# Sliding-window attention and a gated MLP in one kernel: batches 2 to 7 in two-block runs over all heads, q and k turned by DMA into rings

## The chip, the cores and the metric

The kernel runs on one core of a Trainium2 chip. The metric is the device time of one execution in microseconds; the median of the runs is compared. The engines are named as the profile names them: PE (TensorE, matmuls) with PEld (its weight loads), DVE (VectorE), ACT (ScalarE), POOL (GpSimd) and SP (SyncE, which here only issues DMAs). SP and POOL each issue DMAs in the order of the program, and the same 16 DMA engines move all of them.

## The reference

Eight batches, eight heads, 576 positions, 64 numbers a head. Each position attends to itself and the 63 before it; the result goes through two matrices with h * cos(h) between them.

```python
scores = scale * np.matmul(q, k.transpose(0, 1, 3, 2))      # scale = 1/8
mask = (rel >= 0) & (rel < 64)                              # rel = query position - key position
attn = softmax(np.where(mask, scores, -1e9))
x = np.matmul(attn, v)  # to rows of 512: all heads of a position beside each other, 4608 rows
h = x @ w_in            # 512 x 2048
out = (h * np.cos(h)) @ w_out                               # 2048 x 512
```

Inputs and output are float32; the matmuls run on bf16 copies.

## The kernel before

**Units and tiles.** The 4608 rows of x are worked through in nine tiles of 512 rows (`mt` 0 to 8). A sequence of 576 positions is nine blocks of 64 queries, so a tile is eight blocks and a batch nine. Heads go in pairs: pair p holds heads 2p and 2p + 1 on the lower and upper 64 partitions. A *unit* is (batch b, pair p, block j); its scores are 128 rows (64 queries of each head of the pair) by 128 columns (the block's keys and those of the block before). Up to four units that share a PSUM bank are a *group*.

**A unit's way.** `g_scores` makes the scores in PSUM. `g_max` (DVE) adds the mask, writes s and takes the maximum of each row. `g_exp` (ACT) takes one exponential per unit with the sum beside it. `g_inv` (DVE) takes the reciprocals of a group's sums, `g_norm` (POOL, some on DVE) multiplies and writes bf16 weights `w`. `g_trans` has SP issue a DMA transpose to `wT` (groups in `direct` use TensorE instead). `values` multiplies `wT` with v, 64 matmuls per tile, and `put_x` copies the result out of PSUM to `xT`, the input of the MLP.

**Scores of batches 2 to 7.** One 128x128 matmul for each unit: the weights are a block-diagonal copy of q (`qblocks`: head 0's 64 columns above, head 1's below, zeros elsewhere), so one matmul serves both heads. q therefore needs to be turned (features to partitions) and spread into `qblocks`: `tr_q` turns chunks of 96 rows on TensorE and `put_block` copies twice for each pair, or `turn_q` has SP transpose a chunk and `put_turned` spreads it. `TURNED` says how many of the six chunks of a batch go by DMA: two in batches 4 to 6, six in batch 7, none in 2 and 3. k's six chunks are all turned by SP (`turn_k`). The zeros are set once, by eight DVE memsets in the head. Batches 0 and 1 use pairs of 64x64 matmuls on the plain `qtiles`.

**v.** `load_v` brings 128 rows at a time. A block's values need its own 64 rows of v and the 64 before; the tiles that straddle two loads are made by `spread_v`, two POOL copies per batch (DMAs or DVE in the first batches).

**A tile of the MLP.** First 16 steps of four matmuls (512 columns) make h's sixteen blocks in five PSUM banks in turn; after each, ACT takes `sin` of h + pi/2 and DVE multiplies (`gT`). Then 16 steps of four matmuls make the output, 4 x 128 rows, each accumulated over 16 blocks; the copies of the results (DVE, ACT, DVE, ACT) go to `out_sb`, and SP stores 256 rows (512 KB) at a time. The first three blocks of h are interleaved over the four pairs (`skewed`), so that h can begin when pair 0 of xT is there.

**What sets the order.** A tile has T = 32 plan units, one for each step of four matmuls; the first half makes h, the second the output. `at(time, step)` puts a step on the plan, and `pump(time)` emits everything due so far between two steps of matmuls. Each engine then runs its instructions in the order of emission and waits by semaphores. Tile 0 and the loads before it are written out by hand in `FIRST`.

**Where attention stood.** Tile t (1 to 6) does all 36 units of batch t + 1, from plan unit 14.6 on, `PACE` 0.36 units apart per unit of work; `LAGS` gives the due times of the later steps. Within a batch the blocks needed first come first (`CUTS`). The values of tile mt are due 1.01 units before its beginning, those of the last tile 8 units before. q and k for the next batch are loaded in twelve chunks between units 5.6 and 15 of the tile before; k's turns are due from 5.5 units before the tile on, v's loads at 0.5 to 4.5.

**Tables.** Sine and exponential use different ACT tables. `exp_table` loads that of the exponential after the last sine of tiles 1 to 6, the sine's comes with the next sine.

Of the kernel before, what the change touches and what calls it, by code (L numbers as in the profile page):

```python
# [10 lines left out]
def _safe_warn(msg, *a, **kw):  # L11
# [3 lines left out]
F32 = mybir.dt.float32  # L15
# [8 lines left out]
NU = 9  # L24
NC, NP = 6, 96
GF = 4
LAST = 384
PACE = 0.36
CUTS = (
# [6 lines left out]
)  # L36
# [4 lines left out]
LAGS = (0.2, 1, 3, 3.2, 3.8)  # L41
# [5 lines left out]
TURNED = {4: 2, 5: 2, 6: 2, 7: 6}  # L47
# [29 lines left out]
def kernel(  # L77
# [80 lines left out]

    def rows_tile(name):
        return ld.tile([128, NC * H * D], BF16, tag=name, name=name)  # L160

    def load_heads(name, b, p0=0, n=PAIRS):
        if (name, b) not in st:
            st[name, b] = rows_tile(name)[:, 0:PAIRS * RC * D].rearrange("p (a x) -> p a x", a=PAIRS)
# [494 lines left out]
```

## Time and profile before

| | us |
|---|---|
| median of three runs | 309.15 (308.91 to 309.35) |
| span of the profiled execution, first to last instruction | 308.3 |
| PE busy | 298.4 |
| ACT busy | 234.4 |
| DVE busy | 229.3 |
| POOL busy | 192.6 |

The profile is one execution. Its span leaves out what lies before the first and after the last instruction. "Busy" counts the time in which an engine's instructions run; a matmul's end is modelled, so where TensorE's time matters, the chain of work that ended last is used: it goes back from the last instruction, at each step to what released it or to the instruction ahead on its engine, and gives the place in time and the length of each piece. The view by windows gives every engine's busy time in a stretch. In the DMA rows, "to landing" is the time from SP's issue to the last byte's arrival. L numbers are lines of the kernel: L304 is the score matmul of batches 2 to 7, L310 that of batches 0 and 1, L220 the transposes of q on TensorE, L385 the values, L454 the matmuls of h, L619 those of the output, L337 the exponentials, L354 the product with the reciprocals, L368 the DMA transpose of w, L261 and L245 those of k and q, L183 and L189 the loads of q, k and v, L474 the stores. L138 is the line of a helper that makes every copy.

### The profile page before, as it was taken

What the parts mean: (1) busy time and instruction counts of PE and PEld (TensorE: products, weight loads), DVE (VectorE), ACT (ScalarE), POOL (GpSimd) and SP (SyncE); (2) the same over time, 40 slices, a digit from 0 to 9 for tenths busy, and PEclk for the clock granted to TensorE, in tenths of its full rate; (3) what the DMA queues carried; (4) which work ended last, traced back from release to release, by engine and by line L of the source; (5) the groups of instructions that cost most, each with busy time, mean ns of one, the idle gap of its engine ahead of it and who ended that gap; (6) DMA issues with size and microseconds to landing.
All of it is one profiled execution on the core that took longest, in us unless ns stands there. A gap on an engine that the chain in (4) does not pass through costs nothing.

```text
span 308.3 us, 7917 instructions
## 1 busy us (share of the span) xinstructions
PE 298.4 (97%) x2622; PEld 159.0 (52%) x2622; DVE 229.3 (74%) x909; ACT 234.4 (76%) x785; POOL 192.6 (62%) x228
## 2 busy tenths in 40 slices
PE   6978999999999999999999999999999999999996
PEld 3767854544555455445554545455545554454443
DVE  6897988689787976798579866987698768335701
ACT  5897699686997699769976998699869986116600
POOL 7898568996559758967998699949902940000000
PEclk9799999999999999999999999999999999999999
DMA  7999999999999994999999998999794634011011
GB/s 147 180 210 176 198 184 124 117 149 169 233 126 114 153 235 83 100 130 228 153 119 136 215 160 100 156 180 191 90 141 106 162 70 153 2 68 71 0 64 72
DMA packets 159945, 42.14 MB, mean 137 GB/s; under 512 B 148256, under 2 KB 155168, under 8 KB 159904
## 3 DMA queue, kind: packets, MB, share of 16 engines
q0 software_dynamic: 100192, 18.06, 81.9%
q1 hardware_dynamic: 59424, 23.09, 39.8%
q8 instruction: 20, 0.33, 0.5%
q10 hardware_dynamic: 288, 0.49, 0.4%
q14 instruction: 21, 0.17, 0.2%
HBM read 36.70 MB, written 9.44 MB: 150 GB/s over the span
## 4 chain that ended last, share of the span: by engine, by line
PE 88%; POOL 3%; DMA 3%; DVE 2%; ACT 2%; issue 1%; POOLq 0%; DVEq 0%; ACTq 0%
PE h_ps L454 35%; PE out_ps L619 35%; PE s_ps L304 4%; PE h_ps L418 4%; PE out_ps L437 4%; PE o_ps L385 3%; DMA k<-in_k_dram 3%; PE tq_ps L220 1%; PE out_ps L466 1%; ACT e L337 1%; POOL w L354 1%; POOL q L166 1%; DVE v L138 1%; PE s_ps L310 1%; PE tw_ps L365 1%
## 5 line engine op out<-in xcount | busy, mean ns | idle before, releaser
L619 PE MATMUL out_ps<-w_out,gT 128*128 128x512 bf16 x496 | 117.3, 379 | 0.0
L454 PE MATMUL h_ps<-xT,w_in 128*128 128x512 bf16 x512 | 115.3, 379 | 0.2
L605 ACT ACTIVATE sin<-h_ps 128x512 f32<-128x512 f32 x128 | 73.7, 598 | 32.7 <-PE h_ps L454 31.9
L608 DVE TENSOR_TENSOR gT<-h_ps,sin 128x512 bf16<-128x512 f32 x128 | 82.1, 685 | 21.9 <-ACT sin L605 21.2
L337 ACT ACTIVATE e<-s,negm 128x128 f32<-128x128 f32 (+1 forms) x256 | 97.1, 382 | 0.6 <-DVE negm L325 0.6
L354 POOL TENSOR_TENSOR w<-e,rden 128x512 bf16<-128x512 f32 (+1 forms) x74 | 70.2, 963 | 36.7 <-DVE rden L347 30.6
L454 PEld LDWEIGHTS <-w_in 128*128 128x128 bf16 x512 | 48.8, 98 | 54.8 <-issue 0.4
L619 PEld LDWEIGHTS <-gT 128*128 128x128 bf16 x496 | 45.9, 98 | 44.3
L325 DVE CUSTOM_DVE_ANT_0 s<-s_ps,mask 128x128 f32<-128x128 f32 (+1 forms) x256 | 56.4, 278 | 1.8 <-PE s_ps L310 0.9
L337 ACT ACTIVATION_READ_ACCUMULATOR e<-s,negm 128x1 f32 x256 | 48.1, 188 | 0.0
L189 POOL DMA_DIRECT2D v<-in_v_dram x40 | 34.4, 879 | 0.2 <-issue 0.2
L183 POOL DMA_DIRECT2D q<-in_q_dram x36 | 28.3, 785 | 8.9 <-DMA v<-in_v_dram 3.2
L183 POOL DMA_DIRECT2D k<-in_k_dram x36 | 28.0, 779 | 6.2 <-DMA k<-in_k_dram 3.0
L138 ACT COPY out_sb<-out_ps 128x512 f32<-128x512 f32 (+1 forms) x18 | 10.2, 565 | 24.5 <-PE out_ps L619 18.4
L347 DVE RECIPROCAL rden<-den 128x4 f32<-128x4 f32 (+1 forms) x79 | 13.1, 166 | 18.8 <-ACT e L337 18.5
L304 PEld LDWEIGHTS <-qB 128*128 128x128 bf16 x216 | 16.4, 98 | 14.2
L138 DVE CAST xT<-o_ps 128x512 bf16<-128x512 f32 x24 | 15.5, 677 | 10.2 <-PE o_ps L385 10.2
L138 DVE COPY out_sb<-out_ps 128x512 f32<-128x512 f32 x18 | 12.4, 690 | 13.2 <-PE out_ps L619 12.5
L304 PE MATMUL s_ps<-kT,qB 128*128 128x128 bf16 (+1 forms) x216 | 21.3, 217 | 0.0
L325 DVE DVE_READ_ACCUMULATOR2_ANT negm<- 128x1 f32 x256 | 21.3, 83 | 0.0
L138 POOL COPY v<-v 64x1536 bf16<-64x1536 bf16 (+3 forms) x12 | 18.8, 1570 | 0.3
L138 DVE COPY qB<-tq_ps 64x384 bf16<-64x384 bf16 (+1 forms) x40 | 15.5, 388 | 0.4
(73 smaller groups left out, 260.2 us busy)
## 6 DMA issues: line engine op xcount, KB each, us to landing
out_dram<-out_sb SPq DMA_DIRECT2D x16, 512.0 KB, 7.5
v<-in_v_dram POOLq DMA_DIRECT2D x32, 128.0 KB, 6.1
q<-in_q_dram POOLq DMA_DIRECT2D x36, 96.0 KB, 8.7
k<-in_k_dram POOLq DMA_DIRECT2D x36, 96.0 KB, 8.7
w_in<-in_moe_w_in_dram POOLq DMA_DIRECT2D x4, 512.0 KB, 9.1
w_out<-in_moe_w_out_dram POOLq DMA_DIRECT2D x4, 512.0 KB, 10.7
wT<-w SPq DMA_TRANSPOSE x68, 4.2
q<-in_q_dram POOLq DMA_DIRECT2D x7, 144.0 KB, 6.1
```

The costliest lines, as they stand in the source:

```text
L138: {"a": nc.scalar.copy, "p": nc.gpsimd.tensor_copy}.get(engine, nc.vector.tensor_copy)(out, in_)
L183: nc.gpsimd.dma_start(out=st[name, b][:, c].rearrange("p (h d) -> p h d", h=H), in_=src.rearrange("h p d -> p h d"))
L189: nc.gpsimd.dma_start(out=vt.rearrange("p (h d) -> p h d", h=H), in_=v[b, :, c * 128:c * 128 + n, :].rearrange("h p d -> p h d"))
L304: nc.tensor.matmul(out=s_ps[:, u, 0:64 * chunks].rearrange("p (a t) -> p a t", a=chunks), lhsT=qblocks[(b % 2) * PAIRS + p][:, j].rearrang ...
L325: nc.vector.tensor_tensor_reduce(out=s[:, u, c], in0=s_ps[:, u, c], in1=mask[:, 2 - j % 2 if j else 0, c], scale=-scale if b else -1.0, sc ...
L337: nc.scalar.activation(e[:, u, c], s[:, u, c], AF.Exp, bias=negm[:, u:u + 1], scale=1.0 if n < n_first else -1.0, accum_out=den[:, u:u + 1])
L347: nc.vector.reciprocal(out=rden[:, 0:len(groups[n])], in_=den[:, 0:len(groups[n])])
L354: (nc.gpsimd if engine == "p" else nc.vector).tensor_tensor(out=w[:, 0:u], in0=e[:, 0:u], op=ALU.mult, in1=rden[:, 0:u].unsqueeze(2).to_br ...
L454: nc.tensor.matmul(out=st["h", ff], lhsT=w_in_sb[:, ks, ff * 128:ff * 128 + 128], rhs=st["xT", mt][:, ks], start=start, stop=stop)
L605: nc.scalar.activation(sin, h_ps, AF.Sin, bias=math.pi / 2.0)
L608: nc.vector.tensor_tensor(out=gt[:, e], in0=h_ps, in1=sin, op=ALU.mult)
L619: nc.tensor.matmul(out=o_ps[e], lhsT=gT[ff // 2][:, ff % 2, ms * 128:ms * 128 + 128], rhs=w_out_sb[:, ff], start=ff == 0, stop=ff == n_ff - 1)
```

## The change

From batch 2 on the work is counted in *runs*: run r is the two blocks 2r and 2r + 1, counted through all batches, for all four pairs, so eight units. Tile t (1 to 7) does four runs, 32 units, from run 9 + 4(t - 1) on; tile 7 does the last three. The three first of a tile's runs are the last ones that the next tile's values need.

- q and k come in loads of 128 rows (`load_run`, two of 64 rows where a run crosses into the next batch), the next tile's eight in every tile, in six buffers each. SP turns each of them by DMA (`turn_run`) into `qring` and `kring`, which hold nine runs and are written over in turn. No q of these batches is turned on TensorE, and there is no block-diagonal copy any more: `qblocks`, its memsets, `put_block` and `put_turned` are gone.
- The scores of a run are two groups: pairs 0 and 2, pairs 1 and 3. `g_quads` makes both at once: for each of four units, four matmuls with 64x64 weights, one on each quarter of the array: head 0 and head 1 of the one pair to the lower and upper rows of the first bank, head 1 and head 0 of the other pair to the lower and upper rows of the second bank. So pairs 1 and 3 have their heads swapped, and `values` takes them swapped. The two banks come from the three-buffer pool `ps_t`, not from the h banks.
- v also has a ring, in 128-row loads, and a second one (`vW`) for the windows that straddle two loads, filled by two POOL copies per tile.
- The values of pairs 0 and 2 are due 2.05 units before the end of a tile, those of 1 and 3 1.05 units before; h takes the pairs in the order 0, 2, 1, 3. This also holds for the last tile.
- The sine's table is loaded ahead of h's matmuls by a step of its own, the exponential's after tile 7's sines too.
- In `FIRST` the memsets are gone, and the loads for batch 2 are runs 9 to 12.

```diff
+RING = 2 * NU
+RUN0, RUNS = 9, 4
+PAIR_ORDER = (0, 2, 1, 3)
+VALUES = (2.05, 1.05)
+SCORES = (11, 16.4, 19.4, 22.4)
+EXPS = tuple(15.6 + 1.6 * k for k in range(8))
+LAGS = (0.5, 1.9, 2, 3.4)
...
+    qring = const.tile([128, PAIRS, RING * 64], BF16, name="qT")
+    kring = const.tile([128, PAIRS, RING * 64], BF16, name="kT")
+    vD = const.tile([128, RING // 2, d_model], BF16, name="v")
+    vW = const.tile([128, RING // 2 - 1, d_model], BF16, name="vW")
...
+    def load_run(name, r):
+        st["run", name, r] = rows = ld.tile([128, H * D], BF16, tag="r" + name, name="r" + name, bufs=6)
+        load_rows({"q": q, "k": k}[name], rows, r)
+
+    def turn_run(name, r):
+        at_ = 128 * (r % NU)
+        nc.sync.dma_start(out={"q": qring, "k": kring}[name][:, :, at_:at_ + 128], in_=st.pop(("run", name, r)), transpose=True)
...
+    for r in range(RUN0, n_mt * TU // 2):
+        groups += [[(*divmod(g, NU)[:1], p, g % NU) for p in ps_ for g in (2 * r, 2 * r + 1)] for ps_ in ((0, 2), (1, 3))]
...
+    def g_quads(n):
+        banks = [ps_t.tile([128, GF, 128], F32, tag="t", name="s_ps") for _ in range(2)]
+        for u in range(GF):
+            for i, h, to in ((0, 0, 0), (0, 1, 1), (1, 1, 0), (1, 0, 1)):
+                b, p, j = groups[n + i][u]
+                d, e = slice(64 * h, 64 * h + 64), slice(64 * to, 64 * to + 64)
+                nc.tensor.matmul(out=s_of(banks[i][e, u], b, j), lhsT=q_of(b, p, j)[d], rhs=k_of(b, p, j)[d],
+                                 start=True, stop=True, skip_group_check=True)
+        st["s", n], st["s", n + 1] = banks
...
-            if b > 1:
-                nc.tensor.matmul(out=s_ps[:, u, 0:64 * chunks].rearrange("p (a t) -> p a t", a=chunks),
-                                 lhsT=qblocks[(b % 2) * PAIRS + p][:, j].rearrange("d h t -> d (h t)"), rhs=rhs,
-                                 start=True, stop=True, skip_group_check=True)
...
+                of = 1 - h if b >= 2 and p % 2 else h
                 nc.tensor.matmul(out=o_ps[64 * h:64 * h + 64, 64 * i:64 * i + 64],
+                                 lhsT=window(b, j)[:, 128 * p + 64 * h:128 * p + 64 * h + 64],
+                                 rhs=wT[:, 64 * of:64 * of + 64], start=True, stop=True, skip_group_check=True)
...
+    for t in range(1, B):
+        t0 = T * t
+        runs = [RUN0 + RUNS * (t - 1) + i for i in range(RUNS) if RUN0 + RUNS * (t - 1) + i < n_mt * TU // 2]
+        for i, r in enumerate(runs):
+            at(t0 + 0.5 + 2.5 * i, turn_run, "k", r)
+            at(t0 + 0.5 + 2.5 * i + 1.2, turn_run, "q", r)
+            at(t0 + 0.5 + i, load_v, r)
+            at(t0 + SCORES[i], g_quads, n)
+            for e in range(2):
+                k_ = 2 * i + e
+                at(t0 + SCORES[i] + LAGS[0] + 0.5 * e, g_max, n)
+                at(t0 + EXPS[k_], g_exp, n)
+                for lag, fn in zip(LAGS[1:], (g_inv, g_norm, g_trans)):
+                    at(t0 + EXPS[k_] + lag, fn, n)
+                n += 1
         for half_ in range(2):
+            at(t0 + 12.5 + 0.1 * half_, spread_v, half_, runs[0], runs[-1] + 1)
+        for i, r in enumerate(r + RUNS for r in runs):
+            if r < n_mt * TU // 2:
+                for e, name in enumerate("kq"):
+                    at(t0 + 4.5 + 1.8 * i + 0.9 * e, load_run, name, r)
     for mt in range(2, n_mt):
+        for i, p in enumerate(PAIR_ORDER):
+            time = T * mt - VALUES[i // 2] + 0.01 * i
+            at(time, values, mt, p)
+            at(time + 0.2, put_x, mt, p, "a" if i == 2 else None)
...
     for mt in range(1, n_mt):
...
+        pump(base - 0.5)
+        if mt > 1:
+            sine_table()
+        for n, ks in enumerate(PAIR_ORDER):
+            skewed(mt, ks, n)
...
-            if ff == n_ff - 1 and mt < B - 1:
+            if ff == n_ff - 1 and mt < B:
                 exp_table()
```

More of the change, by code (lines that the diff above doesn't have):

```diff
@@ L186, in load_v, with load_rows @@
[L186 to L202 removed]
+    def load_rows(of, to, r):
+        blocks = [divmod(g, NU) for g in (2 * r, 2 * r + 1)]
+        if blocks[0][0] == blocks[1][0]:
+            b, j = blocks[0]
+            parts = ((0, 128, b, 64 * j),)
+        else:
+            parts = tuple((64 * i, 64, b, 64 * j) for i, (b, j) in enumerate(blocks))
+        for at_, n, b, s0 in parts:
+            nc.gpsimd.dma_start(out=to[at_:at_ + n].rearrange("p (h d) -> p h d", h=H),
+                                in_=of[b, :, s0:s0 + n, :].rearrange("h p d -> p h d"))
@@ new lines, in load_v, with spread_v @@
+    def load_v(r):
+        load_rows(v, vD[:, r % NU], r)
+    def load_run(name, r):
[4 more added lines that the diff above has]
+        nc.sync.dma_start(out={"q": qring, "k": kring}[name][:, :, at_:at_ + 128], in_=st.pop(("run", name, r)), transpose=True)
+    def spread_v(half, lo, hi, engine="p"):
+        d = slice(64 * half, 64 * half + 64)
+        rs = [r for r in range(lo, hi) if r % NU]
+        while rs:
+            n = 1
+            while n < len(rs) and rs[n] % NU == rs[0] % NU + n:
+                n += 1
+            at_ = rs[0] % NU
+            rs = rs[n:]
+            to, of = vW[d, at_ - 1:at_ - 1 + n], vD[d, at_ - half:at_ - half + n]
+            if engine == "s":
+                nc.sync.dma_start(out=to, in_=of)
+            else:
+                copy(engine, to, of)
@@ L334, in g_exp @@
         den = att.tile([128, GF], F32, tag="den", name="den", bufs=8)
-        for u, (_, _, j) in enumerate(groups[n]):
-            c = slice(0, 128 if j or n < n_first else 64)
+        for u, (b, _, j) in enumerate(groups[n]):
+            c = slice(0, 128) if j or n < n_first else own(b, j)
             nc.scalar.activation(e[:, u, c], s[:, u, c], AF.Exp, bias=negm[:, u:u + 1], scale=1.0 if n < n_first else -1.0,
@@ L342, in g_inv @@
         e, den = st["e", n]
-        for u, (_, _, j) in enumerate(groups[n]):
+        for u, (b, _, j) in enumerate(groups[n]):
             if j == 0 and n >= n_first:
-                nc.vector.memset(e[:, u, 64:128], 0.0)
+                nc.vector.memset(e[:, u, own(b, j + 1)], 0.0)
         rden = att.tile([128, GF], F32, tag="rden", name="rden", bufs=8)
@@ L591 @@
         gT = []
-        for ks in range(PAIRS):
-            pump(max([base - 1] + [time for time, _, fn, args in plan if fn is put_x and args[:2] == (mt, ks)]))
-            skewed(mt, ks, ks)
+        pump(base - 0.5)
[3 more added lines that the diff above has]
+            skewed(mt, ks, n)
         for ff in range(n_ff):
-            for ks in range(PAIRS):
+            for n, ks in enumerate(PAIR_ORDER):
                 if ff >= SKEW:
-                    first(mt, ff, ks, ks == 0, ks == PAIRS - 1)
+                    first(mt, ff, ks, n == 0, n == PAIRS - 1)
             h_ps = st.pop(("h", ff))
```

199 lines of the change are left out of this document (42 added, 157 removed), and 45 rows, old and new, of tables (CUTS, FIRST).

## The prediction

> **What bounds the kernel now.** I read the page first: the busy shares, then the chain of work that ended last.
>
> ```profile
> span 308.3 us, 7917 instructions
> PE 298.4 (97%) x2622; PEld 159.0 (52%) x2622; DVE 229.3 (74%) x909; ACT 234.4 (76%) x785; POOL 192.6 (62%) x228
> ...
> PE 88%; POOL 3%; DMA 3%; DVE 2%; ACT 2%; issue 1%; POOLq 0%; DVEq 0%; ACTq 0%
> ```
>
> TensorE is busy 97% of the span and carries 88% of the chain, so an edit is worth what it takes off TensorE, unless it makes TensorE wait. The view by windows, cut at the tiles' first h matmuls (tiles 1 to 8), shows where the other engines stand.
>
> ```profile
> core 0: us, PE busy (x) PEld busy (x) DVE busy (x) ACT busy (x) POOL busy (x), PEclk, DMA share, GB/s
> 59.30:91.30 32.00, 31.89 (x252) 16.40 (x251) 26.60 (x124) 27.95 (x102) 22.36 (x27) 1.00 1.86 172
> 91.30:123.20 31.90, 31.86 (x253) 16.53 (x253) 25.40 (x116) 27.58 (x96) 25.34 (x30) 1.00 1.46 144
> 123.20:154.80 31.60, 31.60 (x244) 16.19 (x244) 25.45 (x118) 27.33 (x95) 26.66 (x30) 1.00 1.69 152
> 154.80:186.40 31.60, 31.55 (x247) 16.23 (x246) 25.54 (x118) 27.13 (x95) 26.08 (x30) 1.00 1.57 155
> 186.40:217.90 31.50, 31.50 (x244) 16.13 (x244) 25.45 (x118) 27.03 (x95) 26.15 (x30) 1.00 1.69 153
> 217.90:248.80 30.90, 30.85 (x229) 15.55 (x230) 24.21 (x112) 27.12 (x95) 16.93 (x18) 1.00 0.83 127
> 248.80:277.80 29.00, 29.00 (x193) 13.60 (x193) 15.09 (x24) 12.01 (x20) 1.22 (x2) 1.00 0.23 71
> 277.80:305.50 27.70, 27.67 (x144) 13.30 (x142) 12.01 (x18) 10.88 (x19) 0.00 (x0) 1.00 0.12 48
> ```
>
> Tiles 1 to 6 carry attention and last 31 to 32 us; tile 7 carries only values, tile 8 none. The granted clock is 1.00 throughout, so matmul prices carry over. The chain in order of time prices TensorE's pieces.
>
> ```profile
> 42.03 0.48 PE s_ps L310 x14
> 47.77 0.32 PE s_ps L310 x8
> 154.83 2.75 PE h_ps L454 x12
> 157.58 0.17 PE tq_ps L220 x4
> 169.50 0.20 PE s_ps L304 x4
> 175.47 0.17 PE s_ps L304 x3
> 185.22 1.13 PE o_ps L385 x64
> 277.80 13.81 PE h_ps L454 x64
> ```
>
> **The change, part by part.** *MoE matmuls*, unchanged: 64 take 13.81, so 128 take 27.62 per tile.
>
> *Scores.* Tile 4 before: five groups of four and four of three, 9 bursts of about 0.19, together some 1.8 us. After: one burst per run, of 16 matmuls on 64x64 quarters of the array. The nearest rows are batch 1's 64x64 pairs, whose two heads sit on the array's diagonal: 8 take 0.32 and 14 take 0.48, so (0.48 - 0.32)/3 = 0.053 per pair and 0.11 for the burst. Two already run side by side; that all four quarters do is in no row. Ends: four at once, 4 x 0.053 + 0.11 = 0.33 a burst; two at once, 8 x 0.053 + 0.11 = 0.54; one at a time, 0.96. I take 0.33: the value matmuls (64 in 1.13, 18 ns each for 64 columns) already run two different streams through the array's column halves, as the score pairs run two through diagonal quarters. Four runs a tile: 1.3 us. The Trainium skill (TensorEngine Tiling (Array Packing), Tiling Modes) counts 64x64 as four independent tiles and says that a change of mode drains the array; the 0.11 agrees, and its four would give the 0.33.
>
> *Turned q.* Tile 4 loses 16 TensorE transposes, 4 x 0.17 = 0.7 us (tiles 1 and 2 more, tile 6 none). The copies into qB leave VectorE, 15.5 us in 40 of them, 2.6 a tile, beside ten smaller ones:
>
> ```profile
> L138 DVE COPY qB<-tq_ps 64x384 bf16<-64x384 bf16 (+1 forms) x40 | 15.5, 388 | 0.4
> ```
>
>
> *Values.* Still 64 per tile, but in two bursts with four output matmuls between: 1.13 + 0.11 = 1.24. Pairs 0 and 2 come early enough that their xT copies are done before h needs them; so the 2.75 - 2.59 = 0.16 us that h's first twelve lose to this in each tile goes.
>
> TensorE's tile is then 27.62 + 1.32 + 1.24 = 30.2 us. Against the windows: tile 1 saves 1.5 (32.0 with a 0.3 us stall of its own that stays), tiles 2 to 6 save 1.7, 1.4, 1.4, 1.3 and 0.7; tile 7, with three runs, costs 27.62 + 1.0 + 1.24 = 29.85, 0.85 more. Sum: **-7.15**.
>
> *The other engines.* VectorE loses those copies, ScalarE four exponentials (32 units, not 36); both stay below their 25.5 and 27 of now. The eight memsets leave a VectorE that waited for loads in the head: nothing. Table loads come as often as before in tiles 1 to 6 and once more around tile 7, in the waits priced next.
>
> **The wait that comes instead: exponentials to values.** Now the last values of a tile need six of its eight groups in every tile; before, that was so in tile 1 only. Tile 1 shows the way from the sine of the last h matmul to the landing of the sixth group.
>
> ```profile
> 74.47 0.60 ACT L605 ACTIVATE sin<-h_ps 128x512 f32<-128x512 f32 x1 [0.27 <-PE h_ps L454]
> 75.09 1.28 ACT L446 ACT_TABLE_LOAD   x1
> 76.38 0.20 ACT L446 ACTIVATE small<-small 128x1 f32<-128x1 f32 x1
> ...
> 84.49 0.56 ACT L138 COPY out_sb<-out_ps 128x512 f32<-128x512 f32 x1
> 84.95 0.40 ACT L337 ACTIVATE e<-s,negm 128x128 f32<-128x128 f32 x1
> ...
> 86.50 0.39 ACT L337 ACTIVATE e<-s,negm 128x128 f32<-128x128 f32 x1
> ```
>
> ```profile
> 86.63 0.18 DVE L347 RECIPROCAL rden<-den 128x4 f32<-128x4 f32 x1 [0.55 <-ACT e L337]
> ```
>
> ```profile
> 84.87 1.04 POOL L354 TENSOR_TENSOR w<-e,rden 128x512 bf16<-128x512 f32 x1 [0.38 <-DVE rden L347]
> ```
>
> ```profile
> L368 SPq DMA_TRANSPOSE wT<-w x1: 1192/1192/1192, 87.6 to 87.6; - x1
> ...
> DMA to landing us min/median/max: 2.4/2.4/2.4
> ```
>
> ```profile
> 86.70 3.45 PE out_ps L619 x16
> 90.15 1.13 PE o_ps L385 x64
> ```
>
> Sine, table and the small one: 2.1. Six groups of (86.50 - 84.95) = 1.55: 9.3. The copy in between: 0.46 (84.95 - 84.49). Reciprocal and handovers 0.4, product on POOL 1.04 and handover 0.1, transpose 2.4 to landing. Sum **15.8** after the last h matmul. TensorE gets to the second half of the values after 60 output matmuls (16 in 3.45: 12.95), three bursts (1.0), the first half of the values (0.6) and four more (0.86): **15.4**. So it waits 0.4 in tiles 1 to 6; in tile 7, with two bursts, 0.75: together **+3.15**. Behind that wait stand the next tile's h matmuls, so all of it counts. In tile 1 of before the transpose issued at 87.6 landed at 90.0, and values began at 90.15: just in time. The four groups' scores that TensorE did there after the sixth's are what covered it.
>
> **The second wait: turned q at the first scores.** Scores of a tile's first run stand behind 12 blocks of h, 12 x 0.863 = 10.4 us into the tile. Before, k's chunks were issued up to five plan units ahead of the tile; now all turns are due inside it. SP is in order: the last wT of the tile before (it follows eight exponential groups, 2.1 + 8 x 1.55 + 0.46 + 1.5 = 16.5 after the last h, so about when the tile begins), turn k0, the two 512 KB stores, turn q0. At 1.2 a transpose and 0.5 a store q0 is issued 3.6 us in.
>
> ```profile
> L261 SPq DMA_TRANSPOSE kT<-k x4: 1207/1220/1942, 94.1 to 101.4; - x4
> ...
> DMA to landing us min/median/max: 7.0/7.0/7.8
> ```
>
> ```profile
> L261 SPq DMA_TRANSPOSE kT<-k x6: 1194/1231/2062, 63.6 to 71.7; - x6
> ...
> DMA to landing us min/median/max: 6.9/7.6/7.9
> ```
>
> These are turns issued in the same phase (3 to 10 us into tile 2, 4 to 12 into tile 1), while v and the next chunks load; alone a transpose lands in 2.4. Ends: 3.6 + 2.4 = 6.0, no wait; 3.6 + 7.9 = 11.5, 1.1 a tile. I take 6.9, which lands at 10.5 and costs 0.1 a tile, +0.7 in seven: fewer transposes are queued ahead than in those rows. The Trainium skill (DMA: Bandwidth & Descriptors, Queues, rings and completion order) has each DMA engine go round the queue rows packet by packet; 2.4 against 7 agrees.
>
> POOL: its third and fourth loads of a name wait for buffers that the turns of the first two runs free; behind them stand the two spreads of v and the first product. The rows, from the groups by line and form:
>
> ```profile
> L183 POOL DMA_DIRECT2D q<-in_q_dram x36 | 28.3, 785 | 8.9 <-DMA v<-in_v_dram 3.2 <-DMA q<-in_q_dram 2.1 <-PE h_ps L418 1.8
> ...
> L138 POOL COPY v<-v 64x2048 bf16<-64x2048 bf16 x5 | 9.5, 1892 | 0.3
> ```
>
> With q1 turned some 15 us into the tile, a load (0.8 to 0.9) and two spreads (1.89 each) end near 20, two late for the first product; at 1.04 a product, against a group every 1.55, POOL has caught up by the fifth, which is the first that TensorE waits for. So nothing; beyond 15 each us is one more of wait. Per tile POOL has 12 loads instead of 17.
>
> **Sum.** 308.3 - 7.15 + 3.15 + 0.7 = 305.0 us of span. The runs' median, 309.15, lies 0.85 above the span, so **305.9 us**.
>
> **The rivals.**
>
> *A, turns land late (slower).* In every tile the first scores wait for q0. For it: the 6.9 to 7.9 of the rows, and 1 MB of stores issued just ahead of q0. Against: in tile 1 a store stands among the six turns of the row, and none took over 7.9; and there are fewer loads. Decides from a landing of over 6.8 us after issue. At 7.9 it is 1.1 rather than 0.1 in seven tiles: +7, 312.9. Milder, from 7.4, it already ends above 309.8. Chance 0.22.
>
> *B, the quarters run two at a time*, so that the change does not do what it says: 0.21 more a burst. One burst lies before the last h matmul and costs in full; three lie in the 15.4, where 0.4 are swallowed by the wait: 0.45 in tiles 1 to 6, 0.2 in tile 7, +2.9: 308.8. The Trainium skill (TensorE: Matmul & The Clock Gate, Part 3) has weight loads overlap running matmuls only in other row groups, which would split the four so. Against: in the 0.053 per pair, loads into the same row groups are hidden already. Chance 0.10, mostly no change.
>
> *C, no wait appears*: groups with a batch's first block are shorter, and transposes land in 2.3. 308.3 - 7.15 + 0.85 = 302.0. Chance 0.16.
>
> **The numbers.** Forecast 0.52 (its own range 303.5 to 308), A 0.22, B 0.10, C 0.16. Range 302.0 to 312.5: it cuts half of C and the worst of A. The measurement tells about 0.2% (0.6 us) from no change. Faster: forecast, C and a little of B, 0.70; same 0.08; slower 0.22.
>
> **What would show it.** Right: windows of tiles 2 to 6 near 30.7 and tile 7 near 30.7; bursts of 16 in about 0.33 on the chain; a wait of some 0.4 before the values of pairs 1 and 3, ended by wT or, on the chain, by ACT and POOL; L220 and qB gone. Wrong: a TensorE wait for q's or k's transpose before the first scores (A); bursts near 0.54 (B); tiles of 30.2 (C). It would also be wrong if POOL, held by the loads' buffers, ran its fifth and sixth products late, or if transposes at the tile's end no longer landed in 2.4.

## The result, and the profile after

| | before | after |
|---|---|---|
| median of four runs, us | 309.25 (308.91 to 309.68) | 346.85 (345.19 to 350.38) |
| ratio, 95% interval | 1 | 1.1203 (1.1167 to 1.1239) |
| span of the profiled execution, us | 308.3 | 344.8 |
| tiles 1 to 7, first h matmul of tile 1 to that of tile 8, us | 218.5 | 254.6 |

The change makes the kernel 12% slower. The forecast was 305.9, faster; its range ended at 312.5. One of the four executions after, 350.38, was a slow one; the ratio leaves it out. The lines of the changed kernel have other numbers: L261 is the scores of a run, L185 the turns of q and k, L451 the stores, L362 the values, L431 the matmuls of h, L566 those of the output, L173 the loads of q, k and v, L326 the product with the reciprocals, L126 the helper that makes every copy; a run that adds lines shifts some of them (L264 for L261, L567 for L566). q0 and k0 are the q and k of a tile's first run, q1 and k1 those of its second. The page's lines on busy time, on TensorE's granted clock and on the chain that ended last, after:

```profile
PE 303.7 (88%) x2702; PEld 151.0 (44%) x2742; DVE 209.0 (61%) x844; ACT 238.6 (69%) x795; POOL 196.0 (57%) x219
PEclk9999999989997899969996999989996999999999
PE 54%; DMA 28%; ACT 5%; issue 4%; POOL 4%; DVE 4%; SPq 1%; POOLq 0%; DVEq 0%; ACTq 0%
```

TensorE went from 97% to 88% of the span, and DMAs carry 28% of the chain where they carried 3%. The digits of the granted clock fall below 9 at regular distances, about once a tile. The windows of tiles 1 to 7, columns as in the prediction:

```profile
59.25:94.44 35.19, 32.24 (x256) 14.60 (x257) 22.50 (x106) 26.87 (x95) 21.50 (x24) 0.95 1.45 143
94.44:132.46 38.02, 32.38 (x257) 14.83 (x257) 21.63 (x97) 25.85 (x89) 23.05 (x24) 0.91 1.31 126
132.46:169.65 37.19, 32.74 (x257) 14.92 (x257) 21.77 (x97) 25.86 (x89) 22.92 (x27) 0.91 1.29 128
...
207.67:245.08 37.41, 31.99 (x258) 14.60 (x257) 21.72 (x97) 25.86 (x89) 23.11 (x27) 0.95 1.35 128
245.08:282.80 37.72, 32.23 (x256) 14.79 (x257) 21.55 (x97) 25.86 (x89) 21.35 (x22) 0.91 1.11 120
282.80:313.88 31.08, 30.39 (x242) 14.13 (x241) 19.56 (x75) 23.16 (x73) 11.45 (x11) 1.00 0.73 109
```

Tiles 2 to 6 last 37 to 38 us, 5.6 to 6.8 us more than before, and the clock is 0.91 to 0.95 where it was 1.00. Tile 7, which has three runs and loads no q or k, is short. The view of waits names what TensorE waited for (total, times, longest):

```profile
PE s_ps L261 <- DMA qT<-rq: 26.1, 7, 5.1
```

Seven waits for the turned q, one in each tile, at the first scores. The timeline of SP's queue (start, length, instruction) at tile 2's beginning, and then the answer on that one q turn:

```profile
95.41 1.19 SPq L185 DMA_TRANSPOSE kT<-rk  x1
96.71 1.05 SPq L451 DMA_DIRECT2D out_dram<-out_sb  x2
97.86 2.74 SPq L185 DMA_TRANSPOSE qT<-rq  x1
...
```

```profile
L185 SPq DMA_TRANSPOSE qT<-rq x1: 2737/2737/2737, 97.9 to 97.9; - x1
...
  PE s_ps L261: 5.0, 1
...
DMA to landing us min/median/max: 12.1/12.1/12.1
```

The q0 turn is issued 97.86 - 94.44 = 3.4 us into the tile, as the prediction had it (3.6), but lands 12.1 us later. The prediction took 6.9, with 7.9 as its end. In tiles 2 to 6 the chain gives 12.1, 10.8, 12.1, 9.8 and 10.1 us. (In tiles 5 and 6 SP's order is store, k0, store, q0: the first store then goes out over 4 us ahead of q0, not 1.1.) Then the wait's second price, in windows of tile 2 around it (the granted clock is the first of the last three columns):

```profile
100.00:104.50 4.50, 4.50 (x23) 2.06 (x21) 3.81 (x6) 3.17 (x6) 2.42 (x3) 1.00 1.65 248
104.70:109.90 5.20, 0.28 (x2) 0.00 (x0) 1.38 (x2) 0.65 (x2) 0.00 (x0) 0.77 2.16 113
110.00:111.70 1.70, 1.48 (x18) 0.77 (x20) 0.00 (x0) 0.00 (x0) 0.88 (x1) 0.50 1.89 139
111.70:113.40 1.70, 1.70 (x5) 0.61 (x4) 0.39 (x1) 0.60 (x1) 0.78 (x1) 0.50 1.82 140
113.40:114.40 1.00, 1.00 (x4) 0.43 (x3) 1.00 (x10) 0.31 (x1) 0.36 (x2) 0.51 1.40 181
114.40:117.00 2.60, 2.60 (x14) 1.18 (x13) 2.35 (x12) 1.83 (x4) 2.54 (x3) 1.00 1.82 156
```

TensorE is idle for 5 us, its clock falls to one half during the wait, and the matmuls that follow run at that half until 114.4, some 4.5 us after the q has landed: 5 matmuls touch a window of 1.70 us (111.7 to 113.4), where at full clock 23 touch 4.50. Such stretches of half clock (3.4 or 6.8 us, the idle part included) stand in tiles 1 to 6.

**Accounting.** The version below with all turns earlier and both stores behind them does the same work, with the values in the same two places, and has no such wait. The sums of tiles 1 to 6, first of that version, then of the changed kernel:

```profile
sum 186.14, PE 182.83 PEld 85.44 DVE 129.76 ACT 156.17 POOL 134.88; mean PE 30.47 PEld 14.24 DVE 21.63 ACT 26.03 POOL 22.48
sum 223.55, PE 193.84 PEld 88.53 DVE 130.80 ACT 156.16 POOL 134.99; mean PE 32.31 PEld 14.76 DVE 21.80 ACT 26.03 POOL 22.50
```

The changed kernel needs 37.4 us more. Of these 25.7 are the waits (26.1 less 0.4 in tile 7). TensorE's busy time is 11.0 longer for the same matmuls, about 1.8 a tile: these are the slower ones. That leaves 0.7. (Both traces lack the records of the same five or so matmuls of each tile, so their busy times can be compared.)

### The profile page after: what moved, and what is told of

Same layout as the page of the kernel before. It is cut to its first block, busy times and chain, and to the rows that moved or that the text cites. A ratio compares the mean times of both kernels' runs of the same rounds, so it can differ in the third digit from the quotient of the medians.

```text
span 344.8 us, 8056 instructions
## 1 busy us (share of the span) xinstructions
PE 303.7 (88%) x2702; PEld 151.0 (44%) x2742; DVE 209.0 (61%) x844; ACT 238.6 (69%) x795; POOL 196.0 (57%) x219
## 4 chain that ended last, share of the span: by engine, by line
PE 54%; DMA 28%; ACT 5%; issue 4%; POOL 4%; DVE 4%; SPq 1%; POOLq 0%; DVEq 0%; ACTq 0%
PE out_ps L566 26%; DMA qT<-rq 20%; PE h_ps L431 17%; POOL w L326 3%; PE s_ps L261 3%; PE out_ps L414 3%; ACT e L309 3%; DMA v<-in_v_dram 2%; DMA w_out<-in_moe_w_out_dram 2%; PE o_ps L362 2%; DMA k<-in_k_dram 2%; ACT sin L552 2%; DVE s L296 1%; DMA rows<-in_q_dram 1%; PE out_ps L443 1%
## 5 line engine op out<-in xcount | busy, mean ns | idle before, releaser
L431 PE MATMUL h_ps<-xT,w_in 128*128 128x512 bf16 x497 | 122.6, 403 | 2.0 <-issue 1.1
L555 DVE TENSOR_TENSOR gT<-h_ps,sin 128x512 bf16<-128x512 f32 x128 | 84.1, 688 | 62.1 <-ACT sin L552 61.7
L566 PE MATMUL out_ps<-w_out,gT 128*128 128x512 bf16 x475 | 109.6, 379 | 1.6 <-issue 1.3
L326 POOL TENSOR_TENSOR w<-e,rden 128x512 bf16<-128x512 f32 (+1 forms) x69 | 70.8, 1030 | 52.4 <-DVE rden L319 35.4
L431 PEld LDWEIGHTS <-w_in 128*128 128x128 bf16 x512 | 51.7, 103 | 66.8 <-issue 15.7
L566 PEld LDWEIGHTS <-gT 128*128 128x128 bf16 x496 | 46.3, 98 | 54.2
L296 DVE CUSTOM_DVE_ANT_0 s<-s_ps,mask 128x128 f32<-128x128 f32 (+1 forms) x256 | 55.0, 279 | 6.0 <-PE s_ps L261 4.4
L173 POOL DMA_DIRECT2D rq<-in_q_dram x30 | 26.1, 877 | 32.7 <-DMA qT<-rq 29.6
L173 POOL DMA_DIRECT2D rk<-in_k_dram x30 | 26.2, 877 | 18.6 <-DMA kT<-rk 14.1
L261 PE MATMUL s_ps<-kT,qT 64*64 64x128 bf16 (+1 forms) x432 | 11.8, 232 | 26.9 <-DMA qT<-rq 26.1
L319 DVE RECIPROCAL rden<-den 128x4 f32<-128x4 f32 (+1 forms) x73 | 12.2, 168 | 37.2 <-ACT e L309 37.1
L173 POOL DMA_DIRECT2D v<-in_v_dram x40 | 34.1, 872 | 0.3 <-issue 0.3
L126 POOL COPY vW<-v 64x2048 bf16<-64x2048 bf16 (+3 forms) x20 | 26.6, 1343 | 6.2 <-DMA v<-in_v_dram 5.8
L126 ACT COPY out_sb<-out_ps 128x512 f32<-128x512 f32 (+1 forms) x18 | 10.3, 570 | 23.9 <-PE out_ps L566 17.0
L261 PEld LDWEIGHTS <-qT 64*64 64x64 bf16 x432 | 7.3, 113 | 38.0 <-DMA qT<-rq 29.5
L126 DVE CAST xT<-o_ps 128x512 bf16<-128x512 f32 x24 | 15.7, 680 | 5.0 <-PE o_ps L362 4.8
L126 DVE COPY out_sb<-out_ps 128x512 f32<-128x512 f32 x18 | 12.3, 683 | 9.6 <-PE out_ps L566 8.3
L414 PE MATMUL out_ps<-w_out,gT 128*128 128x512 bf16 x60 | 15.1, 380 | 0.4 <-issue 0.3
```

Source lines behind the costliest of these rows:

```text
L126: {"a": nc.scalar.copy, "p": nc.gpsimd.tensor_copy}.get(engine, nc.vector.tensor_copy)(out, in_)
L173: nc.gpsimd.dma_start(out=to[at_:at_ + n].rearrange("p (h d) -> p h d", h=H), in_=of[b, :, s0:s0 + n, :].rearrange("h p d -> p h d"))
L261: nc.tensor.matmul(out=s_of(banks[i][e, u], b, j), lhsT=q_of(b, p, j)[d], rhs=k_of(b, p, j)[d], start=True, stop=True, skip_group_check=True)
L296: nc.vector.tensor_tensor_reduce(out=s[:, u, c], in0=s_ps[:, u, c], in1=mask[:, 2 - (b * NU + j) % 2] if j else mask[:, 0, 0:64], scale=-s ...
L319: nc.vector.reciprocal(out=rden[:, 0:len(groups[n])], in_=den[:, 0:len(groups[n])])
L326: (nc.gpsimd if engine == "p" else nc.vector).tensor_tensor(out=w[:, 0:u], in0=e[:, 0:u], op=ALU.mult, in1=rden[:, 0:u].unsqueeze(2).to_br ...
```

## The experiments

Theory 1: q0 lands late because two 512 KB stores are issued just ahead of it on SP's queue while loads run, and TensorE pays for the wait twice, by idling and by the half clock. Rivals: the loads of the next tile alone make it late (theory 2); the four-quarter bursts or the values cost more than priced (theory 3).

### Stores later

```diff
-                at(base + T + 0.5 + ms0 / 2, store, o_sb, mt, ms0, 0, 2)
+                at(base + T + 9.3 + ms0 / 2, store, o_sb, mt, ms0, 0, 2)
```

> The two 512 KB stores of a tile go behind its eight turns in SP's order instead of between k0 and q0; nothing else moves. Theory 1 (q0's turn is late because 1 MB of stores is ahead of it on the same queue, while loads run beside them): q0 is issued some 1.2 us earlier and lands about 7 us after its issue, as in tile 1 where no store is ahead (7.3), so the first scores of tiles 2 to 6 wait 0 to 1 us instead of 4 to 5.3, no half clock follows, and the time falls from 347 to 308 to 313. Theory 2 (the loads of v and of the next runs alone make it late): q0 still lands 11 to 12 after its issue, a wait of 3 to 4 us stays, 335 to 342.

Measured: 314.32 us (311.29 to 314.75), 1.0183 (1.0166 to 1.0200) of before: a little above what was expected. Some 32 us of the loss of 37.6 are gone by moving two DMA issues of each tile. (The profiled execution, 311.29, is the fastest of the five; where the others lose another 2 to 3 us no trace shows.) Tile 2's q turn and the waits view:

```profile
L185 SPq DMA_TRANSPOSE qT<-rq x1: 1214/1214/1214, 94.9 to 94.9; - x1
...
DMA to landing us min/median/max: 6.0/6.0/6.0
```

```profile
PE s_ps L261 <- DMA qT<-rq: 2.4, 1, 2.4
```

The landing is halved, from 12.1 to 6.0, the issue itself takes 1.2 instead of 2.7 us, and only tile 1's wait is left, where no store stood ahead. The clock is 1.00 throughout. Theory 1 has its first half; tiles 2 to 6 take 30.9 to 31.2 us. This is the first turn of a tile alone: the next three q turns, in tiles 2 to 6, land 7.3 to 9.1 us after their issue although no store of their tile stands ahead of them. They are needed late enough not to be waited for. The landings of all 27 q turns:

```profile
DMA to landing us min/median/max: 2.4/7.9/9.1
```

### Loads of the runs left out

From tile 2 on the runs' loads of q and k are left out and the turns read the rows that tile 1 loaded, so the attention from batch 3's last blocks on is computed from other rows. The stores stay where the change has them.

```diff
+    def keep_run(name, r):
+        st["run", name, r] = st["run", name, r - RUNS]
...
-        nc.sync.dma_start(out={"q": qring, "k": kring}[name][:, :, at_:at_ + 128], in_=st.pop(("run", name, r)), transpose=True)
+        nc.sync.dma_start(out={"q": qring, "k": kring}[name][:, :, at_:at_ + 128], in_=st["run", name, r], transpose=True)
...
-                    at(t0 + 4.5 + 1.8 * i + 0.9 * e, load_run, name, r)
+                    at(t0 + 4.5 + 1.8 * i + 0.9 * e, load_run if t == 1 else keep_run, name, r)
```

> Leaves out the loads of q and k for runs 17 to 35: from tile 2 on the turns read the rows that were loaded in tile 1 again. Stores, turns and the loads of v stay where they are. Theory 1 and theory 2 both expect q0 in tiles 2 to 6 to land as in tile 7, where stores are ahead but only v is loaded (5.9 after its issue): no wait at the first scores but tile 1's 2.2, 303 to 308. Theory 3 (the stores alone, whatever runs beside them): q0 still lands 10 to 12 after its issue and the time stays over 335.

Measured: 325.30 us, ratio 1.0529 (1.0505 to 1.0554). The expectation was missed: q0 still landed 9.1, 9.2 and 9.6 us after issue in tiles 2 to 4, and the first scores still waited:

```profile
PE s_ps L264 <- DMA qT<-rq: 12.6, 7, 2.6
```

Half of the wait goes with the loads and half stays, with the stores and the loads of v; half clock came twice, in tiles 3 and 4. With the stores late and the loads in place no wait was left in tiles 2 to 6, so it takes both to make q0 this late. What the loads do alone shows on the next three q turns of a tile: with late stores and loads they took 7.3 to 9.1 us, here, without loads and behind both stores and q0, 2.4 to 4.9. The landings of all q turns of this run:

```profile
DMA to landing us min/median/max: 2.4/3.9/9.6
```

In the later tiles 5 to 7 of this run q0 took 6.2 to 7.2, and in tile 7 of the changed kernel, in which no q or k is loaded, 5.9, behind both stores too. In these tiles the first store goes out some 4 us ahead of q0, and not 1.1 as in tiles 2 to 4; whether that is what makes them milder was not tested.

### q0 ahead of the stores

```diff
-            at(t0 + 0.5 + 2.5 * i, turn_run, "k", r)
-            at(t0 + 0.5 + 2.5 * i + 1.2, turn_run, "q", r)
+            at(t0 + (0.4 if i == 0 else 0.5 + 2.5 * i), turn_run, "k", r)
+            at(t0 + (0.45 if i == 0 else 0.5 + 2.5 * i + 1.2), turn_run, "q", r)
```

> Only the turn of q's first run goes ahead of the two stores. Theory 1: the first scores of tiles 2 to 6 wait under 1 us; but k1 and q1 are now behind the stores, land 10 to 12 after their issue at 5 to 7 us into the tile, so about 16 to 18, and the second scores (16 us in) wait 0 to 2 us instead: 308 to 318. Theory 2: as now within 3 us less, 340 to 347.

Measured: 325.48 us, ratio 1.0515 (1.0475 to 1.0556), above what was expected. q0 now landed in 5.1 to 7.8 us, but the next run's q, issued behind the stores, took 8.4 to 10.7. TensorE waited for that instead, and for the last weights (half clock came once, in tile 2, at the second kind of wait):

```profile
PE s_ps L261 <- DMA qT<-rq: 6.6, 6, 2.1
PE o_ps L362 <- DMA wT<-w: 6.3, 4, 3.6
```

How a late q turn ends as a wait for the weights stands in the chain of tile 2, pieces in order of time (start, length, what):

```profile
101.67 10.09 DMA qT<-rq
...
112.29 0.87 POOL rq L173
113.16 1.91 POOL vW L126
...
115.12 1.89 POOL vW L126
...
117.09 0.26 POOL w L326
```

The turn frees the buffer that POOL's next load of q waits for; behind that load stand the two spreads of v and the products. The turn landed 17.4 us into the tile (it began at 94.35).

### Work in the place of the idle time

Twenty 128x512 matmuls whose result nobody reads stand ahead of the first scores in tiles 2 to 6: the wait stays, the idling goes.

```diff
+        if first:
+            fill = ps_t.tile([128, 512], F32, tag="t", name="fill_ps")
+            for _ in range(20):
+                nc.tensor.matmul(out=fill, lhsT=w_in_sb[:, 0, 0:128], rhs=w_in_sb[:, 0, 0:512], start=True, stop=True,
+                                 skip_group_check=True)
...
-            at(t0 + SCORES[i], g_quads, n)
+            at(t0 + SCORES[i], g_quads, n, i == 0 and 1 < t < 7)
```

> In tiles 2 to 6, 20 matmuls of 128x512 whose results nobody reads stand ahead of the first scores (4.3 us at full clock), in the time in which TensorE waits for q0. If the h matmuls behind the wait are slow because TensorE stood idle over 3 to 5 us and its clock was halved for some 3.4 us (0.429 us a matmul instead of 0.216, 7 to 10 of them a tile), the granted clock stays at 1.00 in tiles 2 to 6, the waits at the first scores shrink by what the filling takes, and the time falls by 1.5 to 2.5 in each of five tiles, to 335 to 339. If the clock has nothing to do with the idle time, the time stays within 2 us of 347.

Measured: 338.64 us, ratio 1.0975 (1.0931 to 1.1019), as expected: 8.2 us less than the change (7.0 by the two ratios) although TensorE does 100 matmuls more. The clock is 1.00 in tiles 2 to 6, which take 35.2 to 36.3 us instead of 37.2 to 38.0; most of what is left above 31 is the wait, now filled. The only window at half clock is in tile 1, which has no such filler:

```profile
74.80:78.20 3.40, 3.40 (x10) 1.23 (x9) 1.81 (x14) 1.19 (x2) 3.40 (x4) 0.50 1.31 235
```

So the half clock comes from the idling and is worth 7.0/5 to 8.2/5, 1.4 to 1.6 us a tile here, a lower bound, since what the filler adds to the wait is in it. The 1.8 of the accounting fits.

### The first run's turns in the tile before, stores unchanged

```diff
-            at(t0 + 0.5 + 2.5 * i, turn_run, "k", r)
-            at(t0 + 0.5 + 2.5 * i + 1.2, turn_run, "q", r)
+            at(t0 + (-4.9 if i == 0 and t > 1 else 0.5 + 2.5 * i), turn_run, "k", r)
+            at(t0 + (-4.8 if i == 0 and t > 1 else 0.5 + 2.5 * i + 1.2), turn_run, "q", r)
```

> For tiles 2 to 7 the turns of the first run's k and q are due 4.9 and 4.8 plan units before the tile, between the last two transposes of w that the next values need and the two that they don't; stores and all else as in the change. Theory 1 (what costs is that q0's turn is behind two stores and beside the loads): they land in 2.4 to 5 us, long before the first scores; no wait there but tile 1's 2.2 to 2.6. k1 and q1 come right behind the stores, some 3.5 and 5 us into the tile, land 10 to 12 later, 14 to 17, and the second scores (16 in) wait 0 to 1.5 a tile: 308 to 320. A theory that the score bursts themselves or the values cost the time expects 340 and more.

Measured: 323.99 us, ratio 1.0440 (1.0389 to 1.0492), above the expectation. The first q was early (landed 3.5 to 6.7 us after issue); the second, behind the stores, took 9.4 to 10.8 in tiles 2 to 6, and the waits moved there:

```profile
PE s_ps L261 <- DMA qT<-rq: 8.3, 7, 2.4
PE o_ps L362 <- DMA wT<-w: 5.9, 6, 1.2
```

### One store moved

The first store stays ahead of q0, the second goes to 10.3 units into the next tile.

```diff
-                at(base + T + 0.5 + ms0 / 2, store, o_sb, mt, ms0, 0, 2)
+                at(base + T + (10.3 if ms0 else 0.5), store, o_sb, mt, ms0, 0, 2)
```

> Only the second store of a tile goes behind the turns; the first stays between k0 and q0. Theory 1: half the bytes ahead of q0, so it lands about half way between the change (10 to 12 after its issue) and the kernel with both stores late (5.5 to 6.5): 7.5 to 9, the first scores of tiles 2 to 6 wait 1 to 2.5 us, not long enough to halve the clock: 318 to 326. If it is not the stores' bytes but that SP issues them at all (0.5 us each) that delays q0, the wait goes to under 1: 310 to 315.

Measured: 325.39 us, ratio 1.0509 (1.0466 to 1.0553), as expected. But half clock, which the expectation excluded, came twice, in tiles 5 and 6. Tile 2's q turn:

```profile
L185 SPq DMA_TRANSPOSE qT<-rq x1: 2137/2137/2137, 98.2 to 98.2; - x1
...
DMA to landing us min/median/max: 9.3/9.3/9.3
```

With none, one and two stores ahead, q0's landing in tiles 2 to 6 is 5.5 to 6.5, 8.5 to 9.3 and 9.8 to 12.1 us: about 3 us for the first store, and 1.0 to 3.6, tile by tile, for the second.

### All turns earlier, both stores behind them

The first run's turns go into the tile before (for tile 1 into `FIRST`), the others one place forward, the stores to 6.8 and 7.8 units.

```diff
+            if i or t > 1:
+                at(t0 + (-4.9 if i == 0 else 0.5 + 2.5 * (i - 1)), turn_run, "k", r)
+                at(t0 + (-4.8 if i == 0 else 0.5 + 2.5 * (i - 1) + 1.2), turn_run, "q", r)
...
-                at(base + T + 0.5 + ms0 / 2, store, o_sb, mt, ms0, 0, 2)
+                at(base + T + 6.8 + ms0 / 2, store, o_sb, mt, ms0, 0, 2)
```

> As the kernel with the early turns, and also run 9's turns in the written-out first part, the other three runs' turns one place earlier, and the stores behind them (6.8 and 7.8 units in). No transposed q or k is waited for in any tile. What is left of the change: tiles 2 to 7 of 30.7 to 31.1 (bursts of 0.42 with both changes of the array's mode, not 0.33, and about 0.4 of wait for wT), tile 1 about 31: span 305 to 308, time 306 to 309, no clear gain over before's 308.7. The theory that the change without these waits is worth 7 us gives 302 to 303.

Measured: 309.60 us, ratio 1.0012 (0.9985 to 1.0039): the time of the kernel before, a little above the expectation. No wait for q is left in any tile, and with it the loss is gone, so theory 3, that the bursts or the values cost it, falls; tiles 1 to 7 take 31.4, 30.9, 31.2, 31.0, 30.9, 30.9, 30.6.

### The same, with all values in one place

```diff
-VALUES = (2.05, 1.05)
+VALUES = (1.05, 1.05)
```

> The same with all four pairs' values due 1.05 units before the tile's end in one burst, as before the change. One burst of values fewer saves two changes of mode (0.2) and the wait for the first half's wT (0.3 to 0.4); h's first matmuls then wait for the copies of xT (0.2, as before the change): 0.2 to 0.4 a tile, 1 to 3 us less than its twin. If wT was not what the values waited for, no difference.

> The same kernel as early_all_v once more in more rounds, to tell half a per cent: 307.4 to 309.0, ratio 0.993 to 0.998 if the gain of its tiles (30.7 us each, against 31.9 to 30.9 of before in tiles 2 to 6 and 29.0 in tile 7) is real; 1.000 if the first reading was chance.

Measured: 308.13 us, 1.5 less than the version above, as expected; ratio 0.9948 (0.9918 to 0.9978); in five further rounds 308.76, ratio 0.9966 (0.9939 to 0.9992). This beats the kernel before by 0.3 to 0.5%. The windows of tiles 2 and 7 in the further rounds:

```profile
91.18:121.89 30.71, 30.68 (x257) 14.29 (x257) 21.47 (x98) 25.95 (x88) 23.00 (x24) 1.00 1.58 156
...
244.99:275.61 30.62, 30.40 (x240) 14.14 (x240) 19.78 (x76) 23.00 (x72) 11.59 (x11) 1.00 0.72 111
```

TensorE is busy in all but 0.03 us of tile 2, and so in tiles 3, 5 and 6: 30.7 is the work itself, 0.5 above the prediction's 30.2. The chain shows where:

```profile
141.03 0.35 PE s_ps L261 x16
141.38 2.69 PE out_ps L567 x12
144.08 0.35 PE s_ps L261 x16
```

A burst takes 0.35, near the 0.33 predicted; but the 12 output matmuls between two bursts take 2.69 where 12 x 13.81/64 = 2.59. So each of the four bursts costs about 0.1 more beside itself, which the sum left out. That the change between 64x64 and 128x128 work takes it is likely, but was not tested.

### The order of the sixteen matmuls

The version with all values in one place, with the eight matmuls of the one bank issued before the eight of the other.

```diff
-        for u in range(GF):
-            for i, h, to in ((0, 0, 0), (0, 1, 1), (1, 1, 0), (1, 0, 1)):
+        for quads in (((0, 0, 0), (0, 1, 1)), ((1, 1, 0), (1, 0, 1))):
+            for u, (i, h, to) in [(u, quad) for u in range(GF) for quad in quads]:
```

> As early_all_v, but a run's sixteen score matmuls go bank by bank: only the two quarters on the diagonal alternate for the first eight, then the other two. If four quarters run at once and two do so only in this order, a burst takes 8 x 0.055 instead of 4 x 0.055 and is 0.22 longer (0.64 instead of 0.42): 0.9 a tile, 5.9 in 27 bursts, 313 to 314.5, unless the wait for wT takes some of it in. If all four never ran at once (rival B), no difference from early_all_v.

Measured: 308.35 us, ratio 0.9960 (0.9928 to 0.9992); nothing changed, which by the expectation would have meant that the four never run at once. The single records of one burst say otherwise: the first two matmuls of the first bank start at 141.007 and 141.010, the first two of the second bank, issued ninth and tenth, at 141.034 and 141.037 (the ninth is known by its semaphore wait, for the second bank), the next of the first bank at 141.087 and 141.090. The quarters take their matmuls independently of the order of issue, so the edit did not keep two of them idle, and this run does not tell four quarters from two.

### Two quarters only

The version with all values in one place and the first order of matmuls, without the swap: both pairs use the diagonal quarters (and `values` takes them unswapped).

```diff
-            for i, h, to in ((0, 0, 0), (0, 1, 1), (1, 1, 0), (1, 0, 1)):
+            for i, h, to in ((0, 0, 0), (0, 1, 1), (1, 0, 0), (1, 1, 1)):
...
-                of = 1 - h if b >= 2 and p % 2 else h
+                of = h
```

> As early_all_v, but pairs 1 and 3 keep their heads in place, so that all sixteen score matmuls of a run use the two quarters on the diagonal (and the values take the heads unswapped). If four quarters run at once in the change, whatever the order of issue, and the diagonal ones only two at a time, a burst takes 8 x 0.055 instead of 4 x 0.055: 0.22 longer, 0.9 a tile, 5.9 in 27 bursts: span about 312.5, time 313 to 314.5, slower than before. Rival B of the prediction (the four never run at once) expects no difference, 308 to 309.

Measured: 313.14 us, ratio 1.0130 (1.0108 to 1.0152), within what was expected. The chain at the same place:

```profile
141.93 0.64 PE s_ps L261 x16
142.57 2.69 PE out_ps L567 x12
145.26 0.56 PE s_ps L261 x16
```

The burst goes from 0.35 to 0.56 or 0.64, and tiles 2 to 6 from 30.7 to 31.5: 0.8 a tile, 0.2 a burst. Four quarters do work at once, and that is worth 0.2 a burst, the difference that the prediction had put between its 0.33 and its 0.54.

## Why the prediction was wrong, and where it was right

- **The step that failed: "The second wait: turned q at the first scores."** It took 6.9 us from issue to landing, ends 2.4 and 7.9, and +0.7 in seven tiles. Measured: 9.8 to 12.1 in tiles 2 to 6, and 26.1 us of waits. The time of the first scores (10.3 us into tile 2; 10.4 was taken) and of q0's issue were right, so only the landing is off. In the rows taken as nearest one turn of ten stood behind one 512 KB store, none behind two. "Fewer transposes are queued ahead" chose a value below rows that were already too mild, and even the end of 7.9 was not the worst of before: four turns of k issued 3 to 9 us into its tile 3, with no store ahead, landed later.

```profile
L261 SPq DMA_TRANSPOSE kT<-k x4: 1220/1270/2278, 126.6 to 132.1; - x4
...
DMA to landing us min/median/max: 8.1/8.6/8.8
```

  The store runs show what was missing: 5.5 to 6.5 without stores, about 3 us more for the first and 1.0 to 3.6 for the second.
- **What no step priced: the half clock.** "The granted clock is 1.00 throughout, so matmul prices carry over" held before, where TensorE was never idle for long in these tiles. After 4 to 5 us of idling it did not hold: some 11 us of slower matmuls, of which the filler took away 7 to 8. A wait was priced at its length alone.
- **Rival A** was the mechanism that came, and its threshold held: beyond 6.8 us each further one is a wait (12.1 - 6.8 = 5.3; the wait was 5.0). Its price was not: 312.9 at a landing of 7.9, against 346.85. (One sum in it is off: 0.5 more in seven tiles, for a landing of 7.4, gives 309.4 and not over 309.8.)
- **TensorE's tile** was undersized by 0.5: 30.7, not 30.2, and 30.9 to 31.2 with the values in two places, as they were priced. Some 0.4 are the 0.1 beside each burst. The prediction set a sum of pieces against measured windows: its pieces for tile 4 before (27.62, 1.8, 0.7, 1.13 and 0.16) make 31.4 where the window has 31.6, so 0.2 of what it called a saving was what the pieces leave out in both kernels. The copies of the turned q, L220 and qB, are gone as said; VectorE has 21.5 us a tile, not 25.5, and this bought nothing.
- **Exponentials to values.** 0.4 in each of tiles 1 to 6 was too much. With late stores, where TensorE comes to the values in time, the waits for wT add up to 0.3 us; in the changed kernel none is listed, perhaps because the late scores hold TensorE up first. With the values in one place 0.4 is left in all, in two waits.
- **POOL at nothing** held with late stores, where q1 came 13 to 14 us into tiles 2 to 6. With q0 ahead of the stores it came at 17.4, and the wait for the weights of which the step warns appeared, 6.3 us in four tiles.
- **The sum without the failed step.** The prediction's terms give 218.5 - 7.15 + 3.15 + 0.7 = 215.2 us for tiles 1 to 7. With the turns in time and the values where the prediction had them, these tiles take 216.8, and 215.7 in the best version. That this comes so near is two errors against each other, which is luck: TensorE's work is 214.8 where 218.5 - 7.15 = 211.35 was taken, its idle time 0.9 where 3.85 was.
- **Rival B** is refuted by the diagonal run, **rival C**'s 30.2 by the tiles of 30.7; that no wait appears, C's other half, is nearly so in the best version, with 0.9 us of idle time in seven tiles.
- **Outside the span** the prediction took 0.85, from the median of three executions and the span of another. Against their own spans all executions of before in the experiments take 1.72 to 1.83 more (308.65 us with a span of 306.9), those of the new kernels 1.72 to 2.15. So the profiled execution of before must have been about 1 us longer than the median; the forecast starts at that span and ends with that median, so it is not harmed.

## What to carry to other kernels

A transpose that TensorE waits for is priced by what is issued ahead of it on its own queue and by the loads that run beside it, not by a typical landing: here 2.4 us alone, 7.3 to 9.1 in the midst of the loads, up to 12.1 behind two stores as well. Look for large stores ahead of it and move them behind it. A wait of 4 to 5 us on TensorE cost some 1.4 to 1.8 us more in slow matmuls afterwards, so price both. When turns are moved ahead of one wait, follow the next one in the queue: two of the runs only handed the lateness on to the second run and, by POOL's buffers, to the values.

## What the runs showed of the hardware that was not expected

- The half clock came in pieces of 3.4 or 6.8 us, and it came up to 1 us after TensorE had begun to work again. In tile 1 a wait of about 2.1 us was enough in the changed kernel and one of 3.3 in the kernel with the filler, while waits of 2.1 to 2.4 in tile 1 of four others brought none. The timeline of TensorE after, then with late stores:

```profile
72.36 0.37 PE L261 MATMUL s_ps<-kT,qT 64*64 64x64 bf16 x16 [2.07 <-DMA qT<-rq]
72.67 5.31 PE L431 MATMUL h_ps<-xT,w_in 128*128 128x512 bf16 x16
```

```profile
72.20 0.37 PE L261 MATMUL s_ps<-kT,qT 64*64 64x64 bf16 x16 [2.44 <-DMA qT<-rq]
72.50 3.63 PE L431 MATMUL h_ps<-xT,w_in 128*128 128x512 bf16 x16
```

  The same 16 h matmuls take 5.31 us after the shorter wait and 3.63 after the longer one. In every trace that has a record of the clock, its changes lie whole multiples of 3.413 us apart (after: 73.42, 76.83, 107.55, 114.38 and so on), and where they lie against the wait is what differs. Cut at that grid, the two waits look so (TensorE's busy time first, the granted clock third from the end; after, then with late stores, whose grid is that of its one change, just behind its last instruction at 310.21):

```profile
70.00:73.42 3.42, 1.35 (x22) 0.64 (x21) 1.39 (x2) 0.66 (x2) 1.14 (x2) 1.00 1.37 150
73.42:76.83 3.41, 3.41 (x10) 1.22 (x9) 2.30 (x18) 1.19 (x2) 3.41 (x4) 0.50 1.26 239
```

```profile
67.87:71.28 3.41, 1.89 (x9) 0.69 (x7) 2.73 (x4) 1.79 (x3) 0.89 (x1) 1.00 1.84 133
71.28:74.70 3.42, 2.50 (x27) 1.26 (x28) 0.50 (x1) 0.86 (x2) 2.01 (x3) 1.00 1.56 241
```

  The shorter wait lies whole in one window, the longer one is split between two. In tiles 1 to 7 of all these traces each of the eleven windows at full clock in which TensorE was busy for under 1.4 us was followed by one at half clock, and none over 1.5; of three between, one was. That is a pattern in the traces; no run moved a wait against the grid on purpose. The Trainium skill (TensorE: Matmul & The Clock Gate, Part 1: The HAM clock gate) has the clock decided by the activity in a free-running window of about 3.4 us. The traces agree with it.
- Matmuls on different quarters of the array start out of the order of issue: those issued ninth and tenth started 27 ns after the first two. The Trainium skill (TensorE: Matmul & The Clock Gate, Part 3: Packing small matmuls — row/col tiling) has matmuls in strict order. The records of this run differ in their starts, and they decide here.
- SP's own issue of a transpose takes 1.2 us as a rule, up to 2.7 with no store ahead (the best version, tile 1) and up to 4.3 behind stores (q0 ahead of the stores, tile 5). A long issue also holds up those behind it.
- The place of tile 1's first h matmul, 59.3 before and after, lay between 58.7 and 61.6 in the profiled executions. A difference of that size lies ahead of tile 1, in the loads and batches 0 and 1, and a comparison of two of these kernels by one span alone can't be trusted to 1%.
